# Batch 0's first loads over two hardware DMA queues, and the last output quarter in two column halves

## The chip, the cores and the metric

The kernel runs on one core of a Trainium2 chip. The metric is the device time of one execution, in microseconds (us). Three runs of the kernel before took 265.37, 265.94 and 267.1 us; the median is 265.94 us. One further execution was taken by the profiler, and all durations below come from it.

## The reference, cut to what matters

For each of 8 batches the reference computes a linear attention over 8 heads, 576 positions and 64 channels, and then a normalised two-layer MLP with a residual, on rows of 512 channels:

```python
q_s = softmax(q, over the 64 channels); k_s = softmax(k, over the 576 positions)
kv  = einsum('bhsd,bhse->bhde', k_s, v)            # one 64x64 matrix per head
x   = einsum('bhsd,bhde->bhse', q_s, kv)           # heads side by side: 576 x 512
xn  = (x - mean) / sqrt(var + 1e-6) * g_ln
out = x + relu(xn @ w_ch1) @ w_ch2                 # w_ch1 512x2048, w_ch2 2048x512
```

All inputs and the output are float32 in HBM. The kernel multiplies in bfloat16.

## The kernel before, in words

Positions are cut in two. The first 512 positions of a batch are its main part, four tiles `t` of 128 rows; the remaining 64 rows of all eight batches together make a ninth group, `C9`, which is processed last. One group goes through attention, the first MLP product (`mm1`) and the second (`mm2`). The program order on each engine is written by hand: `run` takes a list of TensorE steps with weights, and a list of side steps, each with a position; a side step is issued in front of the first TensorE step at which the summed weight has reached its position. Instructions of one engine run in that order, and a wait holds up everything behind it on the same engine.

**The start.** `first_batch` loads batch 0 itself. Before the change SP issues all of it: first `load_q0(0)` (L899, L910), the tiles t = 0 and 1 of q for all eight heads, 512 KB in pieces of 512 bytes; then four loads of 288 KB (L912), one for each pair of heads of k, in pieces of 2304 bytes. ScalarE (ACT) issues one load of 2 KB, the gain vector `g_rows` (L914). GpSimd (POOL) issues v in three loads (L931), the second half of q (L901) and then the first columns of the weight w_ch1, `w_raw` (L92, called from `load_w1`), and w_ch2 behind it. Each of these three engines feeds a DMA queue of its own: in the profile q1 is SP's, q10 is ACT's and q0 is POOL's.

The computation of batch 0 starts with `exp_qt` on ACT (L193), which needs all of q's first half. VectorE (DVE) sums, inverts and scales it (L202, L245, L855). TensorE (PE) transposes (L860), and directly behind the first four transposes stands `g_columns` (L885), a small product that needs `g_rows`. Then come `z0_mm` (L274, sums of exp(k)), `kv0_mm` (L291), `po_half` (L397), the normalisation on DVE (L375) and the transposes whose copies (L984) feed the first `mm1_part` (L451). Between them PE runs products of zeros, `warm` (L793). `mm1_part` also needs the first 256 columns of `w_raw`. On ACT the order is: exp of q, exp of k's pairs 0 and 1 (L266), a copy (L862), exp of pairs 2 and 3.

**Batch 1's attention** is issued inside batch 0's `mm2` steps, which are 128x512 products of weight 1 (L497). At position 106 `kv_all(1)` runs 40 products (L316) and DVE turns them into `kv_sb` (L325, L327); at position 111 `po_x(1, 0)` runs four products `po` (L353) that read `kv_sb`, and DVE's `x_fast` (L383, L375) reads `po`.

**The end.** For `C9`, `last_products` forms the output from seven half-size products in PSUM banks a to e. Its last two are each eight products of 128x256 (L544): tile t = 2 into bank a, tile t = 3 into bank d. Each is scaled and added by one DVE instruction over 256 columns (`stt`, L584) and stored by `store` (L594), which issues two DMAs, one on SP for partitions 0 to 63 and one on ACT for partitions 64 to 127. The last five pairs of stores are issued in this way.

Hardware DMAs take their completion semaphores in turn from a set of eight. When all is done, SP waits for the semaphores one after the other, in the order of their numbers (L1119).

Of the kernel before, what the change touches and what calls it, by code (L numbers as in the profile page):

```python
# [15 lines left out]
ALU = mybir.AluOpType  # L16
# [4 lines left out]
def kernel(  # L21
# [16 lines left out]
    nc = tc.nc  # L38

    B, H, S, D = q.shape  # L40
    DM = H * D
    DH = 4 * DM
    P = 128
    T = 4
    SM = P * T
# [3 lines left out]
    NP = H // 2  # L49
# [109 lines left out]
    eks, eqs, eqTs, xs, xnTs, rstds, tqs = {}, {}, {}, {}, {}, {}, {}  # L159
# [171 lines left out]
    def kv_all(b):  # L331
        kv_mm(b, range(T + 1))
        kv_out(b)
# [92 lines left out]
    hbox = {}  # L426
# [90 lines left out]
    def sum_h(g, i):  # L517

        if g == 0 and i == 0:
            hbox["s"] = mlp.tile([P, 4, KH, 2 * P], BF16, tag="hs", name="hs", bufs=1)  # L520
        ks = slice(KH // 2 * g, KH // 2 * g + KH // 2)
        s1, s2, s3, s4 = [hbox["s"][:, n, ks] for n in range(4)]
        a11, a12, a21, a22 = [h_part(odd, half, ks) for half in range(2) for odd in range(2)]
        dst, x, y, op = (
            (s1, a21, a22, ALU.add), (s2, s1, a11, ALU.subtract),
            (s3, a11, a21, ALU.subtract), (s4, a12, s2, ALU.subtract),
        )[i]
        nc.vector.tensor_tensor(out=dst, in0=x, in1=y, op=op)  # L528

    def prod(n, bank, t, k, first=False, own=False):  # L530

        at = slice(t * P, t * P + P)
        if n in (1, 2, 4):
            odd, half = ((0, 0), (1, 0), None, (1, 1))[n - 1]
            lhsT = hbox["h"][:, 2 * k + odd, 2 * half + t, :]
        else:
            lhsT = hbox["s"][:, {5: 0, 6: 1, 7: 2, 3: 3}[n], k, at]
        if n in (1, 2):
            rhs = w2_sb[:, 2 * k + n - 1, 0:DH2]
        elif n == 3:  # L540
            rhs = w2_sb[:, 2 * k + 1, DH2:DM]
        else:
            rhs = w2_q[:, {5: 0, 6: 1, 7: 2, 4: 3}[n], k]
        nc.tensor.matmul(hbox[bank][:, t], lhsT, rhs, start=first and (own or t == 0) and k == 0,  # L544
                         stop=k == KH - 1, skip_group_check=True)

    def bank(name):
        hbox[name] = mm_ps.tile([P, 2, DH2], FP32, tag="m", name="b" + name)
# [18 lines left out]
    def copy_u(name):  # L567
        hbox[name] = mlp.tile([P, 2, DH2], FP32, tag=name, name=name, bufs=1)
        nc.scalar.copy(hbox[name], hbox["a"])  # L569

    def add_u(dst, src):
        nc.vector.tensor_tensor(out=hbox[dst], in0=hbox["b"], in1=hbox[src], op=ALU.add)

    def last_products(product):

        c = C9
        yl = raw.tile([P, T, DM], FP32, tag="qt", name="yl")

        def part(t, col):
            return yl[:, t, DH2 * col : DH2 * col + DH2]  # L580

        def stt(t, col, src, add=None):
            cols = slice(DH2 * col, DH2 * col + DH2)
            nc.vector.scalar_tensor_tensor(  # L584
                part(t, col), in0=src, scalar=rstds[c][:, t : t + 1],
                in1=xs[c][0][:, t, cols] if add is None else add, op0=ALU.mult, op1=ALU.add,
            )

        def store(t0, tn, col):
            cols = slice(DH2 * col, DH2 * col + DH2)  # L590
            for half, eng in enumerate((nc.sync, nc.scalar)):
                ps = slice(64 * half, 64 * half + 64)
                to = out[2 * t0 + half : 2 * (t0 + tn) - 1 + half : 2, SM:S, cols]
                eng.dma_start(to.transpose([1, 0, 2]), yl[ps, t0 : t0 + tn, cols])  # L594

        def both(name, t0, col, add=False):
            for t in range(2):
                stt(t0 + t, col, hbox[name][:, t], part(t0 + t, col) if add else None)

        def own_bank():  # L600
            bank("d")

        def seed_e():
            bank("e")
            add_u("e", "s2")

        product(1, "a", first=True, cut=6, at={
            0: [lambda: sum_h(1, 0), lambda: sum_h(1, 1)],
            15: [lambda: both("a", 0, 0)]})
        product(2, "c", first=True, at={7: [lambda g=g: sum_h(g, 2) for g in range(2)],  # L610
            15: [lambda: both("c", 0, 0, True), lambda: store(0, 2, 0)]})
        product(6, "a", at={7: [lambda g=g: sum_h(g, 3) for g in range(2)], 15: [lambda: copy_u("s2")]})
        product(5, "b", first=True)
        product(7, "a", at={1: [seed_e, lambda: both("b", 2, 1)], 15: [
            lambda: both("a", 2, 1, True), lambda: stt(3, 0, hbox["a"][:, 1]),
            lambda: store(2, 2, 1)]})
        product(3, "e", at={15: [lambda: both("e", 0, 1), lambda: store(0, 2, 1), own_bank]})
        product(4, "a", ts=(0,), at={7: [lambda: stt(2, 0, hbox["a"][:, 0]), lambda: store(2, 1, 0)]})
        product(4, "d", ts=(1,), own=True, at={
            15: [lambda: stt(3, 0, hbox["d"][:, 1], part(3, 0)), lambda: store(3, 1, 0)]})  # L620

    def mm2_fast(c):

        steps = []

        def product(n, name, first=False, at=None, ts=range(2), own=False, cut=None):
            at = at or {}
            order = [(t, k) for t in ts for k in range(KH)]
            if cut:
                order = [(t, k) for ks in (range(cut), range(cut, KH)) for t in ts for k in ks]  # L630
            for i, (t, k) in enumerate(order):

                def go(t=t, k=k, i=i):
                    if i == 0 and first:
                        bank(name)
                    prod(n, name, t, k, first or own, own)
                    for fn in at.get(i + KH * ts[0], []):
                        fn()

                steps.append((0.5, go))  # L640

        def seed_c():
            bank("c")
            nc.scalar.copy(hbox["c"], hbox["a"])

        def seed_e():
            bank("e")
            add_u("e", "s2")

        if c == C9:  # L650
            last_products(product)
            return steps

        def ys(name, col, t0):
            return [lambda t=t: y_quarter(c, t0 + t, col, hbox[name][:, t]) for t in range(2)]

        def sums(*which):
            return [lambda g=g, i=i: sum_h(g, i) for g, i in which if g or c == FAST or i > 1]

        product(1, "a", first=True, cut=6, at={  # L660
            0: sums((1, 0), (0, 1), (1, 1)),
            15: [seed_c]})
        product(5, "b", first=True, cut=4, at={
            8: sums((0, 2), (1, 2))})
        product(6, "a", at={
            8: sums((0, 3), (1, 3)), 15: [lambda: copy_u("s2")]})
        product(2, "c", at={7: [seed_e]})
        product(7, "a", at={2: ys("c", 0, 0)[:1], 5: ys("c", 0, 0)[1:], 15: [lambda: copy_u("s3")]})
        product(3, "e", at={13: [lambda: add_u("b", "s3")]})
        product(4, "a", at={  # L670
            1: ys("e", 1, 0)[:1], 4: ys("e", 1, 0)[1:],
            7: ys("b", 1, 2)[:1], 10: ys("b", 1, 2)[1:], 15: ys("a", 0, 2)})
        return steps
# [214 lines left out]
    def first_batch():  # L888
# [6 lines left out]
        k0, _, q0 = raws[0]  # L895
        v0 = mlp.tile([P, NP, T0, D], BF16, tag="hs", name="v0", bufs=1)
        raws["v0"] = v0

        def load_q0(half, eng=nc.sync):  # L899
            ts = slice(2 * half, 2 * half + 2)  # L900
            eng.dma_start(  # L901
                q0[:, :, ts],
                q[0, :, 0:SM, :].rearrange("h (p t) d -> p h t d", t=T)[:, :, ts],
            )

        def src0(x, j, jn):
            rows = x[0, 2 * j : 2 * j + 2 * jn].rearrange("h (p t) d -> (h p) (t d)", t=T0)
            return rows.rearrange("(j p) n -> p j n", j=jn)

        load_q0(0)  # L910
        for j in range(NP):
            nc.sync.dma_start(k0[:, j : j + 1].rearrange("p j t d -> p j (t d)"), src0(k, j, 1))  # L912
        raws["g"] = outp.tile([KO1, P], FP32, tag="ot", name="g_rows")
        nc.scalar.dma_start(  # L914
            raws["g"], bass.AP(moe_g_ln.tensor, moe_g_ln.offset, [[P, KO1], [1, P]])
# [110 lines left out]
    with tc.manual_schedule(  # L1026
# [10 lines left out]
        def po_x(c, t):  # L1037
            for i in range(NP):
                po_mm(c, t, i)
            x_fast(c, t)  # L1040
# [24 lines left out]
            + [(103 + 0.4 * j, lambda j=j: cast_v(1, j)) for j in range(2)]  # L1065
            + [(104.5, lambda: prep_kvrem(1))]
            + [(106, lambda: (kv_all(1), start_x(1)))]
            + [(111, lambda: po_x(1, 0)), (113, lambda: po_x(1, 1))]
            + [(116, lambda: po_x(1, 2)), (118, lambda: xn_pT(1, 0, nc.scalar)), (119, lambda: square_sum(1, 0))]
            + [(119.5, lambda: po_x(1, 3)), (123, lambda: xn_pT(1, 1, nc.scalar)), (124, lambda: square_sum(1, 1))]  # L1070
            + [(128, lambda: xn_pT(1, 2, nc.scalar))]
# [52 lines left out]
```

## Time and profile before

| | before |
|---|---|
| three runs, us | 265.37, 265.94, 267.1 |
| the profiled execution's own time, us | 265.6 |
| its span, us | 263.6 |
| PE, DVE, ACT, POOL busy | 98%, 82%, 68%, 29% |
| mean granted TensorE clock | 0.999 |
| first product of `mm1` starts at, us | 15.24 |
| last DVE instruction ends at, us | 259.93 |

The span runs from the first to the last instruction; the profiled execution's own time is 2.0 us longer. The times of single instructions are counted from the start of the span. The end of a matmul is modelled, so the distance from one matmul to the next in a run of equal ones is the better measure of what one costs. "Idle before, releaser" tells how long an engine stood still before an instruction, and what came last of the things that it waited for.

### The profile page before, as it was taken

The numbers are of one execution on the slowest core, as the hardware profiler recorded it, in microseconds if no ns is written. First come the engines' busy times: TensorE is split into PE (matmuls) and PEld (weight loads), VectorE is DVE, ScalarE is ACT, GpSimd is POOL, SyncE is SP. The second block draws the span as 40 slices with busy tenths as digits, with TensorE's granted clock in tenths as the row PEclk, the third lists the DMA queues.
The fourth block names the chain that finished last, engine by engine and source line by source line (L and its number), as shares of the span: only waits on it lengthen the run. The fifth ranks groups of instructions, "written<-read, shape, count | busy, mean of one in ns | idle before, by whom it ended". The sixth has DMA issues, their size and how long they took to land.

```text
span 263.6 us, 6818 instructions
## 1 busy us (share of the span) xinstructions
PE 257.4 (98%) x2708; PEld 218.1 (83%) x2711; DVE 217.4 (82%) x475; ACT 178.8 (68%) x350; POOL 76.0 (29%) x126
## 2 busy tenths in 40 slices
PE   8989999999999999999999999999999999999993
PEld 5778855775988998899889988998899888888882
DVE  4667797968989997989798979997999889877873
ACT  4467852896966888688868886788678377438400
POOL 8652316203049007600760076008200300030000
PEclk9999999999999999999999999999999999999999
DMA  6999999997986995799879957997804620521014
GB/s 219 256 204 208 338 208 315 271 155 233 207 151 197 325 136 97 197 308 155 93 215 298 139 99 237 297 135 146 256 6 79 161 82 12 71 90 72 0 42 119
DMA packets 69847, 45.00 MB, mean 171 GB/s; under 512 B 41460, under 2 KB 66040, under 8 KB 69816
## 3 DMA queue, kind: packets, MB, share of 16 engines
q1 hardware_dynamic: 48896, 21.76, 39.3%
q0 software_dynamic: 20320, 22.29, 38.9%
q10 hardware_dynamic: 600, 0.53, 0.6%
q8 instruction: 21, 0.34, 0.6%
q14 instruction: 10, 0.08, 0.1%
HBM read 36.70 MB, written 9.44 MB: 175 GB/s over the span
## 4 chain that ended last, share of the span: by engine, by line
PE 92%; DMA 4%; POOL 2%; issue 0%; ACT 0%; DVE 0%; POOLq 0%
PE ba L544 21%; PE bx L688 19%; PE bb L688 9%; PE ph L451 8%; PE bb L544 5%; PE be L544 5%; PE bc L544 5%; PE pc L497 5%; PE bc L688 5%; DMA w_raw<-in_moe_w_ch_dram 4%; PE ph L436 3%; PE po L353 3%; PE pkv L316 2%; PE ptr L860 1%; POOL v L931 1%; PE po L360 1%
## 5 line engine op out<-in xcount | busy, mean ns | idle before, releaser
L544 PEld LDWEIGHTS <-hs 128*128 128x128 bf16 x512 | 49.5, 98 | 5.7
L688 PEld LDWEIGHTS <-w_q 128*128 128x128 bf16 x448 | 43.1, 98 | 5.2 <-issue 0.2
L544 PEld LDWEIGHTS <-hT 128*128 128x128 bf16 x384 | 37.2, 98 | 4.4
L240 POOL TENSOR_TENSOR tq<-xnT 128x256 bf16<-128x256 bf16 x20 | 12.9, 661 | 78.6 <-DMA xnT<-xn 47.2
L688 PEld LDWEIGHTS <-w1g 128*128 128x128 bf16 x336 | 32.2, 98 | 3.9
L544 PE MATMUL ba<-w_q,hs 128*128 128x256 bf16 x256 | 31.7, 273 | 0.0
L688 PE MATMUL bx<-tq,w_q 128*128 128x256 bf16 x224 | 29.0, 273 | 0.0
L561 POOL DMA_DIRECT2D out_dram<-ot x28 | 15.3, 557 | 46.4 <-DVE ot L555 46.4
L367 ACT ACTIVATE scrap<-x,mv 128x512 bf16<-128x512 bf16 x36 | 25.9, 719 | 1.7 <-DVE x L383 1.3
L383 DVE SCALAR_TENSOR_TENSOR x<-po,rq 128x512 bf16<-128x512 f32 x34 | 23.3, 685 | 1.2 <-PE po L353 1.1
L712 ACT COPY bc<-bx 128x512 f32<-128x512 f32 x28 | 15.2, 594 | 13.0 <-PE bx L688 13.0
L719 DVE TENSOR_TENSOR bb<-bx,s 128x512 f32<-128x512 f32 x28 | 18.2, 694 | 6.3 <-ACT s L716 6.3
L730 ACT ACTIVATE hT<-bc 128x512 bf16<-128x512 f32 x28 | 15.3, 595 | 11.9 <-PE bc L688 11.9
L202 DVE TENSOR_REDUCE zq<-eq 128x16 f32<-128x1024 bf16 (+1 forms) x20 | 20.6, 1049 | 2.3 <-ACT eq L193 2.3
L528 DVE TENSOR_TENSOR hs<-hT 128x1024 bf16<-128x1024 bf16 x32 | 20.9, 674 | 0.9 <-ACT hT L730 0.5
L730 ACT ACTIVATE hT<-bb 128x512 bf16<-128x512 f32 x28 | 15.2, 595 | 8.8 <-PE bb L688 8.8
L353 PE MATMUL po<-kv_sb,eqT 128*128 128x128 bf16 x120 | 20.5, 219 | 0.0
L722 DVE TENSOR_TENSOR hT<-bx,s 128x512 bf16<-128x512 f32 x28 | 18.0, 684 | 3.0 <-PE bx L688 3.0
L569 ACT COPY s<-ba 128x512 f32<-128x512 f32 x15 | 8.7, 579 | 12.5 <-PE ba L544 7.8
L544 PE MATMUL ba<-w_sb,hT 128*128 128x256 bf16 x128 | 16.7, 273 | 0.0
L544 PE MATMUL bb<-w_q,hs 128*128 128x256 bf16 x128 | 16.6, 273 | 0.0
L497 PE MATMUL pc<-w_sb,hT 128*128 128x512 bf16 x61 | 15.6, 379 | 0.2
(135 smaller groups left out, 536.9 us busy)
## 6 DMA issues: line engine op xcount, KB each, us to landing
out_dram<-ot POOLq DMA_DIRECT2D x32, 256.0 KB, 5.9
qt<-in_q_dram SPq DMA_DIRECT2D x5, 1024.0 KB, 7.1
kt<-in_k_dram SPq DMA_DIRECT2D x5, 1024.0 KB, 15.0
vt<-in_v_dram POOLq DMA_DIRECT2D x7, 512.0 KB, 14.3
w_sb<-in_moe_w_ch_dram POOLq DMA_DIRECT2D x4, 512.0 KB, 16.1
qt<-in_q_dram POOLq DMA_DIRECT2D x2, 1024.0 KB, 14.8
kt<-in_k_dram POOLq DMA_DIRECT2D x2, 1024.0 KB, 14.3
w_raw<-in_moe_w_ch_dram POOLq DMA_DIRECT2D x3, 512.0 KB, 13.1
```

Of the source, the lines that this page charges most:

```text
L202: nc.vector.reduce_sum(eqs[c][1][:, ts], eqs[c][0][:, ts], axis=AX.X)
L353: nc.tensor.matmul(pobox["p"][:, i * P : i * P + P], eqTs[c][:, t, i, :], kv_sb[:, c, i, :], start=True, stop=True,)
L367: nc.scalar.activation(scrap, x[:, t], AF.Square, bias=mv[:, t, 0:1], scale=-float(DM), accum_out=mv[:, t, 1:2],)
L383: nc.vector.scalar_tensor_tensor(x[:, t].rearrange("p (h d) -> p h d", h=H), in0=pobox[c, t].rearrange("p (h d) -> p h d", h=H), scalar=1. ...
L451: nc.tensor.matmul(ph[:, m % 2, at : at + tn], (w1g if c else w1_sb)[:, ko, m * P : (m + 1) * P], xnTs[c][:, t0 : t0 + tn, ko, :], start=( ...
L497: nc.tensor.matmul(hbox["pc", t], hbox["h"][:, ko, t, :], w2_sb[:, ko, :], start=(ko == 0), stop=(ko == KO2 - 1),)
L528: nc.vector.tensor_tensor(out=dst, in0=x, in1=y, op=op)
L544: nc.tensor.matmul(hbox[bank][:, t], lhsT, rhs, start=first and (own or t == 0) and k == 0, stop=k == KH - 1, skip_group_check=True)
L688: nc.tensor.matmul(dst[:, q], lhsT, rhs, start=first and q == 0 and ko == 0, stop=ko == 1, skip_group_check=True)
L719: nc.vector.tensor_tensor(out=at[g, "b"], in0=at[g, "x"], in1=at[g, "s"], op=ALU.add)
L722: nc.vector.tensor_tensor(out=h_out(g, 1, 1), in0=at[g, "x"], in1=at[g, "s"], op=ALU.add)
L730: nc.scalar.activation(h_out(g, odd, half), at[g, name], AF.Relu)
```

## The change

Three edits. In `first_batch`, q's first half is loaded in two DMAs of four heads each, one on SP's queue and one on ACT's. Each is followed on its queue by two of k's pairs: pairs 0 and 2 on SP, pairs 1 and 3 on ACT. `g_rows` stays on ACT's queue and is now the fourth DMA there. In `last_products`, the last eight products of 128x256 become sixteen of 128x128: eight for the first 128 columns into bank d, eight for the second 128 into a new bank f, and one DVE instruction over 128 columns for each. The store behind them is as before. In batch 0's list of side steps, `po_x(1, 0)` moves from position 111 to 111.7, which puts one product of `mm2` in front of it that stood behind it.

```diff
-    def prod(n, bank, t, k, first=False, own=False):
+    def prod(n, bank, t, k, first=False, own=False, ch=None):
...
-        nc.tensor.matmul(hbox[bank][:, t], lhsT, rhs, start=first and (own or t == 0) and k == 0,
+        dst = hbox[bank][:, t]
+        if ch is not None:
+            cols = slice(P * ch, P * ch + P)
+            dst, rhs = dst[:, cols], rhs[:, cols]
+        nc.tensor.matmul(dst, lhsT, rhs, start=first and (own or t == 0) and k == 0,
...
+        def last_half(half):
+            cols = slice(P * half, P * half + P)
+            nc.vector.scalar_tensor_tensor(
+                yl[:, T - 1, cols], in0=hbox["df"[half]][:, 1, cols], scalar=rstds[c][:, T - 1 : T],
+                in1=yl[:, T - 1, cols], op0=ALU.mult, op1=ALU.add,
+            )
...
-        product(4, "d", ts=(1,), own=True, at={
-            15: [lambda: stt(3, 0, hbox["d"][:, 1], part(3, 0)), lambda: store(3, 1, 0)]})
+        product(4, "d", ts=(1,), own=True, half=0, at={15: [lambda: last_half(0)]})
+        product(4, "f", ts=(1,), own=True, half=1, at={15: [lambda: last_half(1), lambda: store(3, 1, 0)]})
...
-        load_q0(0)
-        for j in range(NP):
-            nc.sync.dma_start(k0[:, j : j + 1].rearrange("p j t d -> p j (t d)"), src0(k, j, 1))
+        for half, eng in enumerate((nc.sync, nc.scalar)):
+            load_q0(0, eng, slice(4 * half, 4 * half + 4))
+            for j in range(half, NP, 2):
+                eng.dma_start(k0[:, j : j + 1].rearrange("p j t d -> p j (t d)"), src0(k, j, 1))
...
-            + [(111, lambda: po_x(1, 0)), (113, lambda: po_x(1, 1))]
+            + [(111.7, lambda: po_x(1, 0)), (113, lambda: po_x(1, 1))]
```

Left out: `load_q0` takes a slice of heads, the steps of a half product weigh 0.25 in place of 0.5, and `own_bank` opens bank f too. The order of instructions on DVE, POOL and PE is the same as before but for the places named.

More of the change, by code (lines that the diff above doesn't have):

```diff
@@ L601, in own_bank @@
             bank("d")
+            bank("f")
         def seed_e():
@@ L618, in last_products, with product @@
         product(4, "a", ts=(0,), at={7: [lambda: stt(2, 0, hbox["a"][:, 0]), lambda: store(2, 1, 0)]})
-        product(4, "d", ts=(1,), own=True, at={
-            15: [lambda: stt(3, 0, hbox["d"][:, 1], part(3, 0)), lambda: store(3, 1, 0)]})
+        product(4, "d", ts=(1,), own=True, half=0, at={15: [lambda: last_half(0)]})
+        product(4, "f", ts=(1,), own=True, half=1, at={15: [lambda: last_half(1), lambda: store(3, 1, 0)]})
     def mm2_fast(c):
         steps = []
-        def product(n, name, first=False, at=None, ts=range(2), own=False, cut=None):
+        def product(n, name, first=False, at=None, ts=range(2), own=False, cut=None, half=None):
             at = at or {}
@@ L635, in go @@
                         bank(name)
-                    prod(n, name, t, k, first or own, own)
+                    prod(n, name, t, k, first or own, own, half)
                     for fn in at.get(i + KH * ts[0], []):
                         fn()
-                steps.append((0.5, go))
+                steps.append((0.5 if half is None else 0.25, go))
         def seed_c():
@@ L897, in first_batch, with load_q0 @@
         raws["v0"] = v0
-        def load_q0(half, eng=nc.sync):
+        def load_q0(half, eng, hs=slice(0, H)):
             ts = slice(2 * half, 2 * half + 2)
             eng.dma_start(
-                q0[:, :, ts],
-                q[0, :, 0:SM, :].rearrange("h (p t) d -> p h t d", t=T)[:, :, ts],
+                q0[:, hs, ts],
+                q[0, hs, 0:SM, :].rearrange("h (p t) d -> p h t d", t=T)[:, :, ts],
             )
```

## The prediction

> **What bounds the kernel now.** First the page's busy times: PE is the engine that never stands still.
>
> ```profile
> PE 257.4 (98%) x2708; PEld 218.1 (83%) x2711; DVE 217.4 (82%) x475; ACT 178.8 (68%) x350; POOL 76.0 (29%) x126
> ```
>
> So the edits can only move the start of PE's dense stretch, its few holes and the tail behind it. Then the chain that ended last, for the first 16 us (start, us, what):
>
> ```profile
> 5.78 9.41 DMA w_raw<-in_moe_w_ch_dram
> 15.19 0.06 issue
> 15.24 0.73 PE ph L451 x8
> ```
>
> The start is held by a DMA on POOL's queue, not by q and k: `w_raw` is issued at 5.78 and lands at 15.19. The timeline shows how close the chain of q and k is behind it:
>
> ```profile
> 0.78 0.57 ACTq L914 DMA_DIRECT2D g_rows<-in_moe_g_ln_dram  x1
> ...
> 5.09 1.15 ACT L193 ACTIVATE eq<-qt 128x512 bf16<-128x512 f32 x2 [3.06 <-DMA qt<-in_q_dram]
> ...
> 7.78 0.38 PE L885 MATMUL gcp<-ident_f,g_rows 4*128 4x4 f32 x2
> ...
> 14.67 0.76 DVE L984 TENSOR_TENSOR xnT<-ptr,g_col 128x256 bf16<-128x256 bf16 x2 [0.29 <-PE ptr L983]
> ```
>
> ACT waits 3.06 us for q; ten us later the two copies L984 end at about 15.05 and 15.43. The first `mm1` products need the first copy and `w_raw`, the next two need the second copy. Both chains thus end within 0.25 us of each other; an earlier q alone buys nothing past that. For the hole at batch 1's `po`, the timeline again:
>
> ```profile
> 43.07 0.86 DVE L327 TENSOR_TENSOR kv_sb<-pkv,rzk 64x256 bf16<-64x256 f32 x2
> ...
> 43.98 0.38 PE L353 MATMUL po<-kv_sb,eqT 128*128 128x128 bf16 x4
> ```
>
> `kv_sb` is ready at 43.93 and `po` starts at 43.98. For the tail, the operations on `yl` (min/median/max ns, first and last start):
>
> ```profile
> L594 SPq DMA_DIRECT2D out_dram<-yl x5: 534/597/659, 251.9 to 260.0; - x5
> L594 ACTq DMA_DIRECT2D out_dram<-yl x5: 554/643/810, 251.9 to 260.2; - x5
> ...
> L584 DVE SCALAR_TENSOR_TENSOR yl<-bd,rstd,yl x1: 483/483/483, 259.5 to 259.5; 128x256 f32<-128x256 f32 x1
> ```
>
> The last DVE result is there at 259.93. SP issues its last store then, at 259.96; ACT only at 260.25, because its issue before began at 259.34 and took the 810 ns.
>
> **Edit 1, the loads.** Bytes stay the same; the number of HW DMAs rises by one. SP's issues shrink from 5 to 3 (q 0.47 us, k 1.98 us for four), ACT's grow from 1 to 4. At 0.57 us (its row) to 0.81 us (ACT's slowest store issue) each, ACT is done at 3.1 to 4.0 us, before q lets it start at 5.09: hidden, with 1 us to spare, and lost from there on if q came that early. SP's freed second is worth nothing: q's issue was first anyway and k's DMAs queue behind q.
>
> What can move q is the rate at which descriptors reach the DMA engines. By 1-us windows the engines' share is 0.51 (137 GB/s) from 2 to 3 us, and 1.08 (329 GB/s) from 3 to 4. If two queues fed twice as fast, 137 KB more would move in that us: at 329 GB/s, 0.4 us earlier for q. Since POOL's queue has 6 packets from 6 to 7 us and 133 from 7 to 8, its work begins where q1's ends, so `w_raw` could follow by as much. Gain bound: -0.4. If both queues are fed by one source in turn, q lands when it did: 0. The nearest rows are the stores, issued on SP and ACT within 0.01 us of each other (packets, MB, share, in two windows, 253.1 to 253.8 and 253.8 to 254.4):
>
> ```profile
> q1 hardware_dynamic: 108, 0.11, 81.4%
> ```
>
> ```profile
> q10 hardware_dynamic: 144, 0.13, 62.8%
> q1 hardware_dynamic: 36, 0.02, 18.3%
> ```
>
> No packet of ACT's goes out until SP's are nearly through, and the same at 258.1 and 259.8. I take 0.
>
> The Trainium skill (DMA: Bandwidth & Descriptors, "Issuing engines are not separate DMA queues") says that starting DMAs from several engines saves only the sequencer's time for starting them. By that rule this term is 0; without it, by the windows, -0.4. The store rows agree with the rule.
>
> The order within the pairs changes little: pairs 0 and 1 share the time in which they landed one by one, at 5.8 and 6.6; exp of pair 0 began at 6.15. If both land at 6.6, ACT does both exps by 7.95, and the copy behind them began at 7.89: nothing to 0.1.
>
> `g_rows` is the edit's risk. Its packets went first (six between 1.5 and 2.0 us); now they stand behind half of q and two pairs of k on q10. Needed at 7.78 by L885, behind which stand the `warm` products, `z0`, the transposes of tile 1 and `kv0` on an in-order PE that is busy without a hole until 12.3 us; DVE's g_col and the second eqT wait for that too. The four k loads take 4.6 to 6.3 us to land, the last (issued at 2.8) at 9.1. So `g_rows` costs between 0 and 1.3 us. q1 drops from 175 packets in the us from 6 to 49 in the us from 7, so most engines are through by 7.0, and 2 KB uses few of them. I take 0, lands at about 7.5.
>
> **Edit 2, position 111.7.** Equal `mm2` products follow each other at 0.217 us (eight in 1.73). The last before `po` starts at 43.62, so PE is free at 43.84 and stands 0.14 us until 43.98. One more product covers 43.84 to 44.06: -0.14. `po` then comes 0.08 late; DVE's `x_fast` moves from 44.40 to 44.48 and its normalisation from 45.49 to 45.57, while the transposes that read it start at 46.16. If that cover of 0.6 were gone, 0.08 would come back.
>
> **Edit 3, the last quarter.** PE: 128x256 products follow at 0.110 us ((1.04 - 0.27)/7), 128x128 ones at 0.056 (sixteen L451 in 1.06, less 0.22, over 15): 16 x 0.056 against 8 x 0.110 is +0.02. The bank f is one more wait on PE's own earlier work, with nothing behind it but these products. DVE: 256 columns take 0.48 us; a PSUM read of 4 columns 0.15 to 0.18 (L886, L325); in between lies about 0.32 for 128. The first half's instruction runs from 259.06, when DVE is free, to 259.4, beside PE's second half. So the last result comes at 259.93 - 0.16 + 0.02 = 259.79.
>
> What is late next: SP's issue before ends at 259.86, so SP gains 0.06 at most; ACT's last issue stays at 260.25, since it waits for its own issue before. It gains nothing. The two last stores take 2.3 and 2.2 us to land: 262.26 on SP, 262.45 on ACT. The end is then SP's row of waits, eight at 0.06 us. It now begins with the semaphore that q's load and SP's last store share, at 262.26, and passes ACT's, last in the row, at 262.69 without waiting. With one HW DMA more at the start, the turn of eight moves by one: ACT's last store comes to share q's semaphore, and the row begins at 262.45: +0.2. Bounds: -0.1 (all stores 0.1 earlier, no new order) and +0.2. I take +0.2, since both landing times are rows.
>
> **Sum:** 0 - 0.14 + 0.2 = +0.06. On the profiled execution's own time (265.6: span 263.6 and 2.0 around it) that is 265.7; the median, 265.94, lies 0.34 above it and would give 266.0. I write **265.8**. A measurement of this kernel tells about 1% (2.7 us) from no change; the three runs alone span 1.7.
>
> **Rivals.**
> A, the forecast, 0.5: starts and stalls as above; its own range 265.2 to 266.4.
> B, faster by half a us, 0.25: the two queues are fed side by side. For it: the share of 0.51 shows engines starved for descriptors. Against it: the stores. -0.4 - 0.14 + 0.1 is -0.44: 265.2 on the execution's scale, 265.5 on the median's.
> C, slower, 0.2: `g_rows` lands behind k3 and blocks PE at L885. For it: the order on q10, and k3's landing at 9.1. Against it: only four rows of 512 bytes, and engines mostly empty at 7. It decides from a landing past 7.8; each tenth past that shows whole, since PE has no hole behind it and `w_raw` gives cover of 0.15 us only. With 0.8 us late, +0.65 + 0.06: 266.3 to 266.7.
> D, the split does what its words say, within A and B: the last store leaves 0.14 earlier on both queues. Then the tail gives -0.14 in place of +0.2, and A would be 265.3. The 810 ns of ACT's issue speak against it.
> Left over, 0.05: a load late enough to stall `mm1` again.
>
> **Numbers.** B's low end with the tail of D, 264.9 on the lower scale; C's 0.8 with the upper scale and some more, 266.9. That holds A, B and most of C: 264.9 to 266.9. All of the cases lie within 1%: same 0.92. Over 1% faster needs 2.7 us, which no term has: 0.03. Over 1% slower needs twice C's bound: 0.05.
>
> **What would show it.** In the changed profile: q waited for until about 5.1 (A) or 4.7 (B); L885 at 7.8 (A) or behind a wait for `g_rows` at 8.1 to 9.1 (C); the first `mm1` product at 15.2, with the wait still on `w_raw`; no idle before L353 at 44; L544's last sixteen in 0.9 us, DVE's last at 259.8 after the shift, and ACT's last issue 0.3 behind SP's. Wrong would be: a start moved by over 0.5 us, a hole in a later batch, or a tail that ends over 0.2 us nearer to the last product.

## The result: slower by 0.3%, and the profile after

The changed kernel takes 266.54 us (median of 22 runs, 265.64 to 267.49); the kernel before took 265.62 us on the same chips (22 runs). The ratio is 1.0031, 95% interval [1.0019, 1.0042]: slower by some 0.8 us. Ratios, here and below, leave out an execution that is over 1.5% above the fastest of its kernel (one of `g_rows` first and one of the late `g_rows` in the kernel before), while medians and ranges hold all of them. The profiled execution of the changed kernel took 266.81 us with a span of 264.7, 1.1 more than the span before.

The page's row of busy times shows no more work: PE is busy for 257.1 us as against 257.4.

```profile
PE 257.1 (97%) x2719; PEld 218.1 (82%) x2719; DVE 217.8 (82%) x476; ACT 178.6 (67%) x350; POOL 75.9 (29%) x126
```

The time is lost in waits, and most of it ahead of 16.2 us. The timeline of the changed kernel (start, us, engine, line, operation; in brackets the idle time before it and what ended it). Its lines L872, L897, L805 and L997 are the L860, L885, L793 and L984 of before.

```profile
2.36 0.58 ACTq L927 DMA_DIRECT2D g_rows<-in_moe_g_ln_dram  x1
...
5.16 1.15 ACT L193 ACTIVATE eq<-qt 128x512 bf16<-128x512 f32 x2 [3.13 <-DMA qt<-in_q_dram]
...
7.53 0.40 PE L872 MATMUL ptr<-ident,eq 128*128 128x128 bf16 x4 [0.56 <-DVE eq L867]
8.50 0.35 PE L897 MATMUL gcp<-ident_f,g_rows 4*128 4x4 f32 x2 [0.58 <-DMA g_rows<-in_moe_g_ln_dram]
...
14.29 0.89 POOL L114 DMA_DIRECT2D kt<-in_k_dram  x1 [0.46 <-PE po L397]
14.59 0.68 DVE L375 TENSOR_SCALAR xn<-x,mv 128x256 bf16<-128x256 bf16 x2
15.58 0.76 DVE L997 TENSOR_TENSOR xnT<-ptr,g_col 128x256 bf16<-128x256 bf16 x2 [0.31 <-PE ptr L996]
16.15 0.73 PE L451 MATMUL ph<-xnT,w_raw 128*128 128x128 bf16 x8 [0.28 <-ACT eq L193]
```

q is there when it was there before: ACT starts at 5.16 (before: 5.09). The transposes start at 7.53 (7.46). Then PE stands before the product of `g_rows` and starts it at 8.50 instead of 7.78. The first product of `mm1` starts at 16.15 instead of 15.24, and 15.24 was itself late: the two kernels below that keep the loads of before (position 111.7 alone, column halves alone) start it at 15.00 and 14.98. The chain that ended last (start, us, what) no longer runs over `w_raw`, which landed at 13.70 this time:

```profile
2.36 6.00 DMA g_rows<-in_moe_g_ln_dram
8.37 0.14 issue
8.50 0.35 PE gcp L897 x2
```

The 2 KB of `g_rows` took 6.0 us from issue to landing.

For the second edit, the timeline of the changed kernel around batch 1's first `po`:

```profile
43.81 1.47 PE L497 MATMUL pc<-w_sb,hT 128*128 128x512 bf16 x6
45.12 0.39 PE L353 MATMUL po<-kv_sb,eqT 128*128 128x128 bf16 x4
```

Six products at 0.217 us each end at 45.11: `po` follows without a hole. Matched instruction by instruction, the changed kernel is 1.06 us behind the other ahead of this place and 0.93 behind it. The lateness grew from 0.91 to 1.06 on the way, by two more normalisations on DVE (L375) that take 0.64 us (at 19.13) and 0.45 us (at 21.59) instead of 0.35, each beside a load issue of POOL.

For the tail, the operations on `yl` (count, then ns min/median/max, first and last start):

```profile
L605 SPq DMA_DIRECT2D out_dram<-yl x5: 547/595/660, 252.8 to 260.9; - x5
L605 ACTq DMA_DIRECT2D out_dram<-yl x5: 567/647/800, 252.8 to 261.2; - x5
...
L588 DVE SCALAR_TENSOR_TENSOR yl<-bd,rstd,yl x1: 352/352/352, 260.0 to 260.0; 128x128 f32<-128x128 f32 x1
L588 DVE SCALAR_TENSOR_TENSOR yl<-bf,rstd,yl x1: 351/351/351, 260.4 to 260.4; 128x128 f32<-128x128 f32 x1
```

The last DVE result is there at 260.76. SP's row of waits starts at 263.36, right behind the last landing on ACT's queue (263.35), and the span ends 3.94 us after DVE's last result; before it was 3.66. ACT's issue ahead of the last one took 800 ns again, and its last issue is 0.3 us behind SP's.

By medians the loss is smaller than in this pair of profiled executions, and it has two groups. 16 of the 22 executions have a mean granted clock of 0.996 to 1.0 and a median of 266.18. The other six stand at 0.990 or 0.991 and take 266.98 to 267.49. None of the executions of the kernel before that were run beside the experiments (95) was below 0.996.

### The profile page after: what moved, and what is told of

Same layout as the page of the kernel before. It is cut to its first block, busy times and chain, and to the rows that moved or that the text cites. A ratio compares the mean times of both kernels' runs of the same rounds, so it can differ in the third digit from the quotient of the medians.

```text
span 264.7 us, 6842 instructions
## 1 busy us (share of the span) xinstructions
PE 257.1 (97%) x2719; PEld 218.1 (82%) x2719; DVE 217.8 (82%) x476; ACT 178.6 (67%) x350; POOL 75.9 (29%) x126
## 4 chain that ended last, share of the span: by engine, by line
PE 93%; DMA 2%; ACT 1%; DVE 1%; ACTq 0%; issue 0%
PE ba L548 21%; PE bx L700 19%; PE bb L700 9%; PE ph L451 7%; PE bb L548 5%; PE be L548 5%; PE bc L548 5%; PE pc L497 5%; PE bc L700 5%; PE ph L436 3%; PE po L353 3%; DMA g_rows<-in_moe_g_ln_dram 2%; PE pkv L316 2%; PE ptr L872 1%; PE warm L805 1%; PE z L274 1%
## 5 line engine op out<-in xcount | busy, mean ns | idle before, releaser
L724 ACT COPY bc<-bx 128x512 f32<-128x512 f32 x28 | 15.2, 594 | 13.0 <-PE bx L700 13.0
L742 ACT ACTIVATE hT<-bb 128x512 bf16<-128x512 f32 x28 | 15.2, 595 | 8.8 <-PE bb L700 8.8
```

The costliest lines, as they stand in the source:

```text
L742: nc.scalar.activation(h_out(g, odd, half), at[g, name], AF.Relu)
```

## Experiments

Two theories stood against each other at first. In the expectations, G is that the late `g_rows` alone makes the loss; S is that the two queues, or the later order of k, cost by themselves. A further question was what the six executions at a lower clock come from.

### The late product taken away: `g_columns` moved behind `kv0_mm`

The changed kernel; PE meets the product of `g_rows` some 4 us later.

```diff
         eq_pT(0, 0, nc.scalar)
-        g_columns()
         exp_k0(2)
...
         for j in range(NP):
             kv0_mm(j)
+        g_columns()
```

> The changed kernel, its loads untouched; only the product that needs g_rows moves on PE from behind the first four transposes to behind kv0_mm, ahead of two warm products. Theory G: g_rows still lands past 8, but nothing stands behind it; first mm1 product at 15.0 to 15.5, ratio 0.999 to 1.0007, the same as with g_rows issued second. Rival S, or a load that hurts by its place on the queue and not by blocking PE: 1.003.

Measured: 265.43 us (11 runs; before 265.51), ratio 0.9995 [0.9979, 1.001], no execution below 0.996. Its timeline:

```profile
7.55 0.40 PE L872 MATMUL ptr<-ident,eq 128*128 128x128 bf16 x4 [1.27 <-DVE eq L867]
...
11.79 0.38 PE L897 MATMUL gcp<-ident_f,g_rows 4*128 4x4 f32 x2
...
15.02 0.87 PE L451 MATMUL ph<-xnT,w_raw 128*128 128x128 bf16 x8 [0.28 <-DVE xnT L997]
```

`g_rows` still landed at 8.01, and no engine waited for it. The two queues are as in the changed kernel, and the loss is gone. S falls.

### The late load taken away: `g_rows` second on ACT's queue

The changed kernel, with `g_rows` issued between q's second four heads and k1.

```diff
         for half, eng in enumerate((nc.sync, nc.scalar)):
             load_q0(0, eng, slice(4 * half, 4 * half + 4))
+            if half:
+                nc.scalar.dma_start(
+                    raws["g"], bass.AP(moe_g_ln.tensor, moe_g_ln.offset, [[P, KO1], [1, P]])
+                )
             for j in range(half, NP, 2):
                 eng.dma_start(k0[:, j : j + 1].rearrange("p j t d -> p j (t d)"), src0(k, j, 1))
-        nc.scalar.dma_start(
-            raws["g"], bass.AP(moe_g_ln.tensor, moe_g_ln.offset, [[P, KO1], [1, P]])
-        )
```

> The changed kernel with g_rows issued on ACT right behind q's second half and ahead of k's pairs 1 and 3. Theory G with descriptors made in the order in which SP and ACT issue: g_rows lands near 5.7, its product starts at 7.5 to 7.9, no hole there, q lands at 5.1 as in the kernel before, first mm1 product at 15.0 to 15.5; ratio 0.999 to 1.0007, and no execution at a granted clock of 0.991 or less. Rival S (two queues cost by themselves): ratio stays at 1.003.

Measured: 265.68 us (12 runs; before 265.51), ratio 1.0003 [0.9987, 1.0019], no execution below 0.996. `g_rows` landed at 4.68. The timeline:

```profile
7.72 0.38 PE L897 MATMUL gcp<-ident_f,g_rows 4*128 4x4 f32 x2
...
15.08 0.73 PE L451 MATMUL ph<-xnT,w_raw 128*128 128x128 bf16 x8 [0.28 <-DVE xnT L998]
```

`g_rows` landed a us earlier than expected: ahead of the k that SP had issued at 1.26, whose parts landed from 5.04 to 5.69. Two edits that share only this, that PE no longer waits for `g_rows`, each bring the kernel level with the one before. G holds.

### The same wait put into the kernel before

The kernel before, with `g_rows` issued by SP behind the four loads of k (`nc.sync` in place of `nc.scalar` in its issue).

> The kernel before with one edit: g_rows is issued on SP behind the four k loads, not on ACT; q and k stay on one queue. Theory G: g_rows lands at 8.0 to 9.3, its product starts that late, the first mm1 product moves from 15.2 to between 15.5 and 16.6, ratio 1.001 to 1.005. Rival S: nothing moves, ratio 1.000.

Measured: 266.05 us (12 runs; before 265.45), ratio 1.0021 [1.0005, 1.0037]. Three of the 12 executions had a clock of 0.986 to 0.991 and took 267.09 to 269.66. The timeline of one at 0.998:

```profile
3.29 0.37 SPq L914 DMA_DIRECT2D g_rows<-in_moe_g_ln_dram  x1
...
8.10 0.35 PE L885 MATMUL gcp<-ident_f,g_rows 4*128 4x4 f32 x2 [0.21 <-DMA g_rows<-in_moe_g_ln_dram]
...
15.43 0.73 PE L451 MATMUL ph<-xnT,w_raw 128*128 128x128 bf16 x8 [0.28 <-DVE xnT L984]
```

`g_rows` landed at 7.96, and like the first `mm1` product that is a little earlier than expected. Against the profile of the kernel before, the product starts 0.32 late and `mm1` 0.19; against the two kernels with `mm1` at 15.00 and 14.98 it is 0.43 to 0.45. The nine executions at 0.997 or more have a median of 265.89, 0.44 above before. So with no other part of the change a `g_rows` behind k costs 0.2% here, and the three executions at a lower clock pay more.

### `g_rows` first on ACT's queue: a miss, and a look at the order of the queues

The changed kernel, with ACT's issue of `g_rows` put ahead of the loop over the two queues.

> The changed kernel with g_rows issued first on ACT's queue, ahead of q's second half. Theory G (all that matters is that g_rows stood behind half of q and two pairs of k): the gain vector's product L885's counterpart starts at 7.8 to 7.9 again, PE has no hole ahead of it, the first mm1 product starts at 15.1 to 15.5, and with -0.13 at position 111.7 and +0.15 in the closing row the total is within 0.3 us of before (ratio 1.000 to 1.001). Rival S (two queues for q and k are themselves slow, whatever stands behind them): first mm1 product near 16.1 and ratio 1.003 as in the changed kernel.

Measured: 267.47 us (11 runs; before 265.45), ratio 1.0072 [1.0036, 1.0108]; slower than the changed kernel, against what G as written there expected. Six of its 11 executions are at a clock of 0.98 to 0.99 and take 267.47 to 271.32, the others 266.06 to 266.57. The timeline of one at 0.983:

```profile
1.26 0.96 SPq L929 DMA_DIRECT2D kt<-in_k_dram  x2
1.39 0.42 ACTq L913 DMA_DIRECT2D qt<-in_q_dram  x1
...
6.56 1.15 ACT L193 ACTIVATE eq<-qt 128x512 bf16<-128x512 f32 x2 [4.54 <-DMA qt<-in_q_dram]
...
8.93 0.40 PE L872 MATMUL ptr<-ident,eq 128*128 128x128 bf16 x4 [1.83 <-DVE eq L867]
...
9.57 1.25 PE L805 MATMUL warm<-junk 128*128 128x256 bf16 x5
```

The issue of `g_rows` pushes that of q's second half from 0.78 to 1.39, behind SP's first k at 1.26. Although the two are on different queues, q's half now lands behind that k: its packets' landings run from 4.93 to 6.47, k0's from 4.06 to 5.22. q is complete 1.4 us later than in the changed kernel for an issue that is 0.6 later. Each landing is recorded in 16 parts: 15 of this half's are there by 5.52, half a us later than in the changed kernel (5.03); the last one, at 6.47, makes up the rest, and why it is late is not shown. The transposes wait, and the second price follows, by the windows (PE, PEld, DVE, ACT, POOL busy, granted clock, DMA share, GB/s):

```profile
10.00:20.00 10.00, 9.35 (x189) 7.42 (x187) 4.11 (x15) 3.79 (x12) 5.67 (x7) 0.68 1.26 224
```

In these 10 us the granted clock is 0.68 on the mean (1.0 in both kernels' profiles): 0.5 from 9.60 to 16.43 us and full on both sides of that. With it, the five `warm` products at 9.57 take 1.25 us instead of 0.72.

### The hole filled: more `warm` products

The changed kernel with 36 products in place of 31 in the first row of `warm`, and seven more ahead of the product of `g_rows`. In the second form all stand in the first row's PSUM tile, so that no tile is added. Both add work and leave nothing out.

```diff
-        warm(31)
+        w0 = warm(36)
...
         eq_pT(0, 0, nc.scalar)
+        warm(7, w=w0)
         g_columns()
```

> The changed kernel with 12 warm products more: 5 behind the first 31 and 7 ahead of the product that needs g_rows, so that PE has no hole at 7 to 8.5, though it still waits for g_rows. Theory C (the executions at a granted clock of 0.990 to 0.991, 6 of 22, pay about 1 us more because PE stood still): no execution at 0.991 or less, first mm1 product still at 16, ratio 1.002 to 1.003. Rival: these executions are not due to the hole; about 3 of 11 are at 0.991 or less again.

> The changed kernel with the warm row lengthened from 31 products to 36 ahead of the transposes and seven more 128x256 products between the transposes and the product of `g_rows`, all in the first row's tile, so that PE has work while it waits for `g_rows`; nothing else moves. Theory that the wait for `g_rows` alone sets the time and that the hole also lowers the granted clock in some executions: with the hole filled no execution is at 0.991 or below, the first product of mm1 stays at about 16.1, the ratio is 1.002 to 1.003. Rival, that the lower clock comes from the later start or from the two queues and not from the hole: about 3 of 11 executions still stand at 0.991 or below and the ratio stays at 1.003 to 1.005.

Measured: 267.59 us (6 runs; before 265.51), ratio 1.007 [1.0047, 1.0092], and 267.56 us (5 runs; before 265.45), ratio 1.0078 [1.0064, 1.0091]. No execution of the 11 was below 0.996, as the hole theory has it; the time missed the expectation by over a us both times. The timeline of the second form:

```profile
14.01 0.71 PE L806 MATMUL warm<-junk 128*128 128x256 bf16 x5
16.00 0.39 PE L806 MATMUL warm<-junk 128*128 128x256 bf16 x2 [1.28 <-issue]
```

PE stops for 1.28 us in the middle of a row of seven equal products that wait for no other engine, and in the first form it stops in the same row (1.26 us, resumed at 15.96). The PSUM tile is thus not the reason. In the DMA view from 13.6 to 14.6 us (queue, kind: packets, MB, share) there is one packet of a kind not yet looked at:

```profile
q8 instruction: 1, 0.02, 5.6%
```

It is 16,384 bytes and starts at 13.67. PE resumes 2.33 us later; in the first form 2.30 us later (13.66, 15.96). The same packet is in every kernel of this study. In three of them (`g_columns` behind `kv0_mm`, and the two of the last experiment) the fourth `mm1` product follows the third by 0.20, 0.11 and 0.24 us where 0.055 is usual, and each time it starts 2.34 to 2.36 us behind the packet. I read it as PE's own code: twelve products more, and PE reached the end of the code that it had. The place of the stop speaks for it: counted in the records from PE's first product, the one that comes late is number 223 in those three kernels, an `mm1` product, and number 224 in these two, a product on `junk`. The reading was not tried by itself; what starts the transfer stays open.

### The hole filled without a product more

The reading above asks for a test that keeps the code's length. The changed kernel, with the five `warm` products that stand behind the product of `g_rows` put ahead of it:

```diff
-        g_columns()
         exp_k0(2)
         warm(5)
+        g_columns()
```

> The changed kernel with one swap in PE's row: the five products on `junk` that stood behind the product of `g_rows` stand ahead of it, and nothing is added, so that PE's code has the length that it had. `g_rows` still lands at 8.0 to 8.4. Theory that the empty wait of PE is the loss, not the late landing as such: the product still starts at about 8.5, but `z`'s first product at about 8.8 and no longer 9.4, the first product of mm1 at 15.2 to 15.5 and no longer 16.15, no execution at a granted clock of 0.991 or below, ratio 0.999 to 1.001. Rival, that what comes later on DVE and POOL with the late product sets the start: first product of mm1 at about 16, ratio about 1.003, 3 of 11 executions at 0.991 or below. A mixed outcome, early start but low clocks, would say that the clock follows something else than the hole.

Measured: 265.57 us (12 runs; before 265.47), ratio 1.0003 [0.999, 1.0017]. The timeline:

```profile
7.59 0.71 PE L805 MATMUL warm<-junk 128*128 128x256 bf16 x5
8.23 0.38 PE L897 MATMUL gcp<-ident_f,g_rows 4*128 4x4 f32 x2
8.54 0.73 PE L274 MATMUL z<-ones,ek 64*64 64x1 bf16 x36
...
14.94 0.73 PE L451 MATMUL ph<-xnT,w_raw 128*128 128x128 bf16 x8 [0.28 <-DMA w_raw<-in_moe_w_ch_dram]
```

`g_rows` lands at about 8.07 and its product runs 0.45 us later than in the kernel before, but PE has something to do until then, and `z` starts at 8.54 (before: 8.75, after: 9.43). `mm1` starts even earlier than the expected 15.2, as early as in the two kernels at 15.00 and 14.98. The loss is gone, although every load is issued as in the changed kernel and `g_rows` lands when the kernel before has long used it. One execution of the 12 still had a clock of 0.990 (267.14 us), against the expectation: the wait for `g_rows` is not the only condition of the lower clock.

### The two other edits, each alone

The kernel before, with nothing but position 111.7 in place of 111:

> The kernel before with only position 111 moved to 111.7. Expected: no hole ahead of po at 44, everything behind it 0.13 to 0.14 us earlier, ratio 0.9995. Rival: the later po holds up DVE's x_fast and the transposes behind it, and the gain is back to 0 by 50 us.

Measured: 265.27 us (12 runs; before 265.45), ratio 1.0 [0.9986, 1.0014]. The timeline shows the hole of 0.14 us closed (five products at 0.217 from 42.81 end at 43.89). The time cannot show it, since 0.14 us is 0.05% and the interval is wider:

```profile
42.81 1.24 PE L497 MATMUL pc<-w_sb,hT 128*128 128x512 bf16 x5
43.89 0.39 PE L353 MATMUL po<-kv_sb,eqT 128*128 128x128 bf16 x4
```

The kernel before, with nothing but the last quarter's column halves:

> The kernel before with only the last eight products in two column halves (loads and position 111 as before). Forecast's step: the last DVE result 0.14 us earlier, SP's last store issue at most 0.06 earlier, ACT's last store issue where it was, because it waits for its own issue before; ratio 0.9998 to 1.000. Rival D: both last stores leave 0.14 earlier, ratio 0.9995.

Measured: 265.49 us (12 runs), ratio 0.9997 [0.9984, 1.001]. The operations on `yl`:

```profile
L605 SPq DMA_DIRECT2D out_dram<-yl x5: 547/596/659, 251.6 to 259.7; - x5
L605 ACTq DMA_DIRECT2D out_dram<-yl x5: 552/647/810, 251.6 to 260.0; - x5
```

SP issues its last store at 259.69, right behind DVE; ACT at 259.99, behind its own issue of 810 ns. From PE's first product of the last quarter to DVE's last result it takes 1.28 us instead of 1.39, but ACT's last store leaves no earlier for it, and the end follows DVE's last result by 3.7 us. The trace speaks against D; the interval of the ratio holds both.

### One hardware DMA more

The kernel before, with a second copy of `g_rows` loaded on ACT into a tile that nobody reads; from one profiled execution.

```diff
+        raws["g2"] = outp.tile([KO1, P], FP32, tag="ot", name="g_rows2")
+        nc.scalar.dma_start(
+            raws["g2"], bass.AP(moe_g_ln.tensor, moe_g_ln.offset, [[P, KO1], [1, P]])
+        )
```

> The kernel before with g_rows loaded a second time on ACT into a tile that nothing reads: one hardware DMA more, all else as before. The step on the closing row: ACT's last store then shares the first semaphore of the row, so the row starts with the later of the two landings, and from the last DVE result to the end of the span it takes 3.8 to 3.9 us in place of 3.66. Rival: the order of the row does not follow the turn of the semaphores; 3.66 again.

Measured: span 263.5 us. DVE's last result is there at 259.65, SP's row of waits starts at 262.18, with ACT's last landing (262.16), and the span ends at 263.52: 3.87 us behind DVE as against 3.66. The 0.2 us of the turned order of semaphores are there without any other edit. The other traces agree: the same distance is 3.87 to 3.94 us in all eight profiles with the additional hardware DMA and 3.62 to 3.78 in the six without.

### Two versions meant to beat both

First, the changed loads with `g_rows` issued by POOL behind v, which takes the additional hardware DMA away again, and `g_columns` behind `kv0_mm`. Second, the loads of before with the two later edits and `g_columns` behind `kv0_mm`.

> The changed kernel with the load of `g_rows` issued on POOL behind v's two, and its product `g_columns` moved behind the first product of k and v; the two queues then carry q and k alone. Theory that the late `g_rows` is the whole loss: product long landed when PE reaches it, first product of mm1 at about 15.0 to 15.2, closing row as before the change, about 265.2, ratio about 0.999. Rival, that the load split has a price of its own: ratio 1.002 or more.

> The kernel before with the position 111.7, the two column halves of the last quarter, and `g_columns` behind the first product of k and v; the loads stay as before. Theory: the two later edits give 0.1 each at most and the product of `g_rows` no longer waits: 265.2 to 265.3, ratio about 0.999. Rival, that moving `g_columns` opens a hole ahead of it in PE's row: 265.7 or more.

Measured: 265.49 us (11 runs; before 265.45), ratio 0.9994 [0.9979, 1.0009], and 265.34 us (11 runs), ratio 0.9994 [0.9985, 1.0003]. Neither is shown to be faster than the kernel before. The timeline of the second shows a part of why an earlier start gives so little:

```profile
14.74 0.92 PE L451 MATMUL ph<-xnT,w_raw 128*128 128x128 bf16 x8 [0.28 <-DVE xnT L996]
```

The first `mm1` product starts 0.5 us earlier than in the profile of the kernel before, and 0.25 earlier than in the two kernels at 15.00 and 14.98, but the eight take 0.92 us instead of 0.73: the fourth comes 0.24 us behind the third, 2.36 us after the packet that I read as PE's code.

## Why the prediction was wrong

- **The forecast** of 265.8 stood for no change that can be told, with half of the chance on it. The kernel is slower by 0.3%, and the measured 266.54 is inside the range and inside rival C's 266.3 to 266.7. C, which had a chance of 0.2, is what happened: `g_rows` lands late on ACT's queue and blocks an in-order PE. The sum came to +0.06, yet the 265.8 lies below the median of the three runs known then, 265.94; over 22 runs the median of before is 265.62, so the choice between the two scales was set by the noise of three runs. The range held the result because its upper end was C's, not because the forecast's mechanism was right.
- **The step that failed** is "`g_rows` costs between 0 and 1.3 us ... I take 0, lands at about 7.5". It landed at 8.02 to 8.36, and the product started 0.72 late. The argument was that q1's packets become few after 7 us and that 2 KB use few engines. That counts the load of the engines; what held `g_rows` is its turn: issued ahead of ACT's two k pairs instead, it landed at 4.68. It was issued at 2.36, as the last of seven loads, and arrived together with the pairs k2 (8.04) and k3 (8.21). The bound of 1.3 had been worked out from the right row, k3's landing; the value taken from inside it was the wrong end.
- **C's price** per late tenth, "shows whole", is right and a little short: 0.72 late became 0.91 at the first `mm1` product. The last 0.2 are in DVE's two normalisations, 0.68 us instead of 0.48, during which POOL issues a load (14.29 to 15.18) that before came later. In both profiles every 128x512 normalisation without such an issue beside it takes 0.35 us, and with one it takes from 0.35 to 0.64. Seen in these traces and not tried.
- **A second price that no step named**: the lower granted clock in six of 22 executions. Their median is 267.17, against 266.18 for the rest.
- **The load split itself at 0** was right, and rival B wrong: ACT starts on q at 5.16 as against 5.09, and the kernels in which `g_rows` does no harm stand at 0.9995 and 1.0003. The rule of the Trainium skill quoted there (DMA: Bandwidth & Descriptors, "Issuing engines are not separate DMA queues") agrees with these numbers.
- **Edit 2 at -0.14** was right: the matched offset falls from 1.06 to 0.93 there, and alone the edit closes the hole.
- **Edit 3** was right in its parts: DVE's instruction over 128 columns takes 0.35 us (0.32 estimated), ACT's last issue does not move and is held by its 800 ns (D is wrong), and the additional hardware DMA costs 0.2, shown alone. In the changed kernel the tail as a whole is 0.15 longer.
- **The start's cover**, "`w_raw` gives cover of 0.15 us only", did not apply: `w_raw` landed at 13.70 in the changed kernel's profile and at 15.19 before. That landing differs from one profile of this study to the next (13.40 to 15.19 with `w_raw` at the same place in POOL's row), and here the other chain decides.

## What to carry to other kernels

A small load that an in-order engine needs early is to be looked at like a big one when loads are dealt out over queues: count the bytes issued ahead of it, on its own queue above all, and take its landing from the landings of its neighbours in issue order, not from the load of the engines. If it must be late, put work that has to be done anyway between it and the place where the engine would stop; here a swap of two lines in PE's order was worth as much as a better place for the load. An edit that adds an early DMA or some twelve products can also cost far from its place, by the order of the completion semaphores at the end and, if the reading above is right, by the code that has to be loaded.

## What the runs showed of the hardware that was not expected

- **Large loads on the two hardware queues landed in the order of issue, across the queues.** A half of q issued at 0.78 completes at 5.07; issued at 1.39, 0.13 us behind a k of the other queue, it completes at 6.47, behind that k. The 2 KB of `g_rows` did not keep that order: issued on ACT at 1.32, it landed at 4.68, ahead of the k that SP had issued at 1.26 (5.69).
- **A hole of PE at the start can lower the clock for what follows.** With an empty wait for `g_rows` or, in one kernel, for q, 15 of 45 executions had a mean granted clock of 0.991 or below; in all other kernels, the one before included, 1 of 188 had (the changed kernel with the swap). Waits ahead of the transposes alone, 0.92 to 1.27 us in the profiles of three kernels, went with none of their 35 executions, so the length of one hole does not decide it. The traces show what goes with it. The recorded clock changes only after whole steps of 3.413 us, and the steps lie differently in each profile: the first one at full clock begins at 4.46 to 7.01 us. In the 14 profiles every step at full clock in which PE stood still for 1.83 us or more in sum is followed by half the clock: 1.83 us with `g_rows` first, and in 14 others, at or behind PE's last product, 2.09 us or more. No step with 1.53 us or less is; in between there is none. In the changed kernel's own profile the two holes of 0.56 and 0.58 us share one step, 1.1 us together, and the clock stays. That the sum came out higher in its six executions at a lower clock is an inference, since none of them was profiled, and the one execution of the swap is not explained. The Trainium skill (TensorE: Matmul & The Clock Gate, "HAM oscillation — how this bites in real kernels") gives gaps of over about 3.4 us as what lowers the clock; here 1.83 us of idle time came ahead of a clock of 0.5, and the measurement decides.
- **PE can stand still where no other engine holds it; its own code is the likely reason.** A 16 KB packet on the instruction queue starts at 12.8 to 13.7 us in all kernels but one. Where PE reaches its 223rd or 224th product early, it stops there until 2.30 to 2.36 us after that; with twelve products more it stood for 1.28 us. The Trainium skill (Runtime: NRT & Kernel Launch, "Instruction fetch mechanics") says that an engine's code is refilled in blocks of 16 KiB over a DMA queue of its own and that the cost of a block is mostly hidden. The size agrees with the packet; the cost was hidden in the kernel before by 0.05 us or so (its fourth `mm1` product comes 2.41 us after the packet), and not hidden in five other kernels.
